# K and V of a batch pooled into one tile and turned in 128x128 shapes, two low weight pieces on GpSimd, another order of the two output scatters of a half block

## The chip, the core and the metric

The kernel runs on one core of a Trainium2 chip. The metric is the device time of one execution in microseconds (us). A core has five engines that work side by side: PE (TensorE, matrix products; its weight loads are shown apart as PEld), DVE (VectorE), ACT (ScalarE), POOL (GpSimd) and SP (SyncE, here only an issuer of transfers). DMA queues carry data between DRAM and the on-chip memory and inside it.

## The reference, cut to what matters

```python
q, k, v = (8, 8, 576, 64) each; moe_w_gate (512, 8), moe_w1 (8, 512, 1024), moe_w2 (8, 1024, 512)
k_p = k.reshape(B, H, 72, 8, D).mean(axis=3)          # 8 neighbours of the sequence pooled
v_p = v.reshape(B, H, 72, 8, D).mean(axis=3)
attn = softmax(q @ k_p^T / sqrt(D));  attn_out = attn @ v_p
x = attn_out.transpose(0, 2, 1, 3).reshape(4608, 512)  # one row per token, heads side by side
logits = x @ w_gate;  expert_idx = argmax(logits);  gate_w = softmax(logits)[expert_idx]
y[tokens of e] = relu(x[tokens of e] @ w1[e]) @ w2[e]  # each token by its one expert
return gate_w[:, None] * y
```

Inputs and output are float32. The kernel computes the products of the experts in pairs of float16 numbers, a high part and a low part (the rest after rounding), with three products for one.

## The kernel before

The program has two halves. The first is the attention with the router. It runs over 36 units of 128 tokens (four to a batch and one shared by the 64 left-over tokens of each pair of batches), in the loop at L1000 to L1045. In unit i the code lays down, in this order for every engine: GpSimd's hook "q"; the transposes of the probabilities (`u_pt`, L524 on PE, copied out by ACT as `pt`, L526); scores of a later unit (`g_s`, L500, or L494 where tokens of two batches meet) and their exponentials (`g_exp`, L517, ACT); transposes of q (`g_qt`, L477, copied by ACT L480); the hooks "pe", "act", "dve"; the product with V (`u_pv`, L546); small steps of the router from a list of fillers; the hooks "dve3", "pe2", "sp"; the moves inside the chip's memory, issued by ACT (L1037); and `u_nrm` (DVE L573, L574, L575), which divides by the sum of the exponentials and writes the token rows `both`. The engines take their instructions in this order, so the place of a hook is a place in a queue.

K and V of batch b are loaded by SP into one of three tiles `kv`, and GpSimd sums each over its 8 neighbours in three additions: 128x1280 (L338), 128x640 (L340), 128x320 (L341). Each L338, and each L340 that is placed alone, waits for the newest "beat", the reciprocal L574 of the unit laid down before (`on_beat`, L316). The table POOLAT gives the units. K then goes through PE (`k_pe`, L379) and ACT (`k_act`, L391) into the score operand `bd`, whose upper and lower 64 partitions hold the same numbers for different heads, so one half is written by ACT and the other is copied from it by a transfer that ACT's queue issues (L1037). V goes two ways: PE turns it (`v_pe`, L403 to L407), ACT copies it (`v_act`), PE multiplies it with the router's weights (`u_pe`, L422, L424), and DVE writes that product (`gates`, L431) and V itself under the mask `mk` (`masked`, L436, two instructions for one batch) into `vb`, the right operand of `u_pv`.

The other steps that the change touches: `lsplit` (L868) writes on DVE the low part of a piece of the first expert's weights, as four instructions of 128x256 for each of eight pieces j, at hook "dve3" of units 13 to 35. The router's rows of a group of four units are scattered by GpSimd to `x_by_expert` in DRAM, sorted by expert (L677, one indirect transfer per unit, held in a list and laid down one by one by `flush`). When the rows of the first 24 units are out, SP loads the first block of 256 rows (L927, unit 29), GpSimd splits it into high and low (L901, L902, unit 30), SP's transposing transfers turn it (L913, unit 31), and PE begins the first block's first product in units 33 to 35 (L987 to L989).

The second half is the expert layer: a loop over blocks of 256 rows (full) or 128 rows (half) of one expert, L1319. At a block's end ACT scales two results of 128 rows (`take`, L1273) and GpSimd scatters them to the output (`give`, L1276 to L1278), row set 1 first and row set 0 second. In a half block, row set 1 has no rows: its row numbers lie outside of the output and nothing is written.

## Time and profile before

| | us |
|---|---|
| median of 3 runs | 592.2 |
| lowest, highest run | 591.74, 595.24 |
| the profiled execution | 594.74 |
| its span, first to last instruction | 592.1 |
| PE busy in the span | 567.0 (96%) |
| DVE busy | 306.5 (52%) |
| ACT busy | 276.4 (47%) |
| POOL busy | 241.4 (41%) |
| mean granted clock of TensorE | 0.987 |

The profile is of one execution. The rows of a timeline give the start and the duration of an instruction or of a run of equal ones (xN), and in brackets how long the engine had been idle before it and what released it. A matmul's duration overlaps with the next one's, so PE's progress is read from starts. ACTq, SPq and POOLq rows are the issuing of transfers, not the transfers.

### The profile page before, as it was taken

What the parts mean: (1) busy time and instruction counts of PE and PEld (TensorE: products, weight loads), DVE (VectorE), ACT (ScalarE), POOL (GpSimd) and SP (SyncE); (2) the same over time, 40 slices, a digit from 0 to 9 for tenths busy, and PEclk for the clock granted to TensorE, in tenths of its full rate; (3) what the DMA queues carried; (4) which work ended last, traced back from release to release, by engine and by line L of the source; (5) the groups of instructions that cost most, each with busy time, mean ns of one, the idle gap of its engine ahead of it and who ended that gap; (6) DMA issues with size and microseconds to landing.
All of it is one profiled execution on the core that took longest, in us unless ns stands there. A gap on an engine that the chain in (4) does not pass through costs nothing. (4 is left out here: it accounts for less than half of the span.)

```text
span 592.1 us, 15018 instructions
## 1 busy us (share of the span) xinstructions
PE 567.0 (96%) x4332; PEld 423.3 (71%) x4333; DVE 306.5 (52%) x639; ACT 276.4 (47%) x627; POOL 241.4 (41%) x465
## 2 busy tenths in 40 slices
PE   7989999999999989999999999999999999999993
PEld 6778998889885755775676676765767657767571
DVE  5776779997798272128312221272313723182783
ACT  4666788878942362227222222261223622272771
POOL 6495889884545222122222012231122311224255
PEclk8998999999999999999999999999999999999998
DMA  9997999857357959952943214339143491319310
GB/s 278 299 313 196 327 336 344 255 173 277 98 187 230 287 154 360 347 123 65 335 134 91 53 58 111 90 66 351 58 111 84 95 352 38 105 35 333 75 45 12
DMA packets 94072, 107.76 MB, mean 182 GB/s; under 512 B 53894, under 2 KB 62086, under 8 KB 94040
## 3 DMA queue, kind: packets, MB, share of 16 engines
q1 hardware_dynamic: 86408, 85.46, 49.6%
q0 software_dynamic: 6640, 20.99, 9.5%
q10 hardware_dynamic: 992, 0.92, 0.6%
q8 instruction: 16, 0.26, 0.2%
q14 instruction: 16, 0.13, 0.1%
HBM read 73.65 MB, written 23.37 MB: 164 GB/s over the span
## 5 line engine op out<-in xcount | busy, mean ns | idle before, releaser
L1067 PEld LDWEIGHTS <-bd 128*128 128x128 f16 x936 | 91.2, 98 | 105.7 <-DVE bd L1061 0.8
L1061 DVE SCALAR_TENSOR_TENSOR bd<-ps,bd 128x512 f16<-128x512 f32 (+1 forms) x44 | 27.5, 630 | 143.7 <-ACT bd L1057 143.2
L1277 POOL TENSOR_TENSOR spacer<-ql,iG 1x1 f32<-1x1 f32 x44 | 18.5, 420 | 166.2 <-ACT ql L1273 154.1
L517 ACT ACTIVATE both<-ps,nmx 128x72 f32<-128x72 f32 x288 | 70.0, 350 | 12.6 <-DVE nmx L510 12.2
L1067 PE MATMUL po<-w,bd 128*128 128x512 f16 x264 | 59.1, 379 | 0.0
L1067 PE MATMUL po<-kv,bd 128*128 128x512 f16 x264 | 58.8, 379 | 0.0
L546 PE MATMUL po<-vb,pt 128*128 128x146 f32 (+1 forms) x320 | 52.7, 311 | 5.5 <-DVE both L575 4.6
L1278 POOL DMA_INDIRECT out_dram<-ql,iG x44 | 47.1, 1071 | 22.0 <-issue 20.6
L1057 ACT ACTIVATE bd<-ps 128x512 f16<-128x512 f32 (+1 forms) x44 | 23.8, 547 | 69.2 <-PE L987 56.4
L546 PEld LDWEIGHTS po<-vb,pt 128*128 128x128 f32 x320 | 46.5, 192 | 8.4 <-issue 5.2
L1067 PE MATMUL pq<-kv,bd 128*128 128x512 f16 x216 | 48.1, 379 | 0.0
L989 PE MATMUL ps<-kv,qt 128*128 128x256 f16 (+1 forms) x176 | 44.8, 263 | 0.9 <-DVE qt L115 0.9
L677 POOL DMA_INDIRECT x_by_expert<-both,rpos x36 | 35.8, 996 | 23.2 <-issue 6.2
L987 PE MATMUL ps<-kv,w 128*128 128x256 f16 (+1 forms) x176 | 43.1, 258 | 2.3 <-DVE bd L906 1.8
L500 PE MATMUL ps<-bd,qT 128*128 128x144 f32 x256 | 45.0, 301 | 0.0
L987 PE MATMUL ps<-kv,qt 128*128 128x256 f16 (+1 forms) x176 | 44.8, 263 | 0.0
L988 PE MATMUL ps<-kv,qt 128*128 128x256 f16 (+1 forms) x176 | 44.8, 263 | 0.0
L989 PE MATMUL ps<-kv,w 128*128 128x256 f16 (+1 forms) x176 | 43.1, 258 | 0.0
L988 PE MATMUL ps<-kv,w 128*128 128x256 f16 (+1 forms) x176 | 43.1, 258 | 0.0
L1067 PE MATMUL pq<-w,bd 128*128 128x512 f16 x192 | 42.7, 379 | 0.0
L338 POOL TENSOR_TENSOR st<-kv 128x1280 f32<-128x1280 f32 x13 | 37.7, 2901 | 12.0 <-DVE ri L574 7.0
L1273 ACT ACTIVATE ql<-po,gB 128x512 f32<-128x512 f32 x22 | 15.1, 685 | 55.5 <-PE L987 41.6
(246 smaller groups left out, 1274.4 us busy)
## 6 DMA issues: line engine op xcount, KB each, us to landing
st<-in_moe_w_dram SPq DMA_DIRECT2D x8, 2048.0 KB, 13.8
both<-in_moe_w_dram SPq DMA_DIRECT2D x6, 2048.0 KB, 12.9
vb<-x_by_expert SPq DMA_DIRECT2D x16, 578.0 KB
kv<-in_v_dram SPq DMA_DIRECT2D x16, 512.0 KB
kv<-in_k_dram SPq DMA_DIRECT2D x7, 1024.0 KB
qt<-in_q_dram SPq DMA_DIRECT2D x7, 1024.0 KB
st<-in_moe_w_dram SPq DMA_DIRECT2D x4, 1024.0 KB
kv<-in_v_dram SPq DMA_DIRECT2D x8, 208.0 KB
```

What stands on the lines that cost most here:

```text
L338: on_beat(nc.gpsimd.tensor_tensor(t1, src[:, :, 0:4 * D], src[:, :, 4 * D:], op=OP.add))
L500: nc.tensor.matmul(ps[:, x * 2 * KP:(x + 1) * 2 * KP], t[:, h, :], BD[b % 3][:, :, h, :], start=True, stop=True)
L517: nc.scalar.activation(p[:, h * KP:(h + 1) * KP], ps[:, x * KP:(x + 1) * KP], AF.Exp, bias=nmx[:, x:x + 1], scale=-1.0)
L546: nc.tensor.matmul(po[:, cols], a[:, c * 128:(c + 1) * 128], VB[b % 3][:, c, sl, 0:CW], start=h in (0, LEFT), stop=False, skip_group_check ...
L677: st = nc.gpsimd.indirect_dma_start(out=xs, out_offset=bass.IndirectOffsetOnAxis(ap=Z["pos"][:, u:u + 1], axis=0), in_=X[:, u, :], in_offs ...
L987: nc.tensor.matmul(dst, wh, xT[:, d, 0:n], start=(d == 0), stop=False)
L988: nc.tensor.matmul(dst, wh, xT[:, DC + d, 0:n], start=False, stop=False)
L989: nc.tensor.matmul(dst, wl, xT[:, d, 0:n], start=False, stop=(d == DC - 1))
L1057: nc.scalar.activation(h, p, AF.Relu)
L1061: V.scalar_tensor_tensor(l, p, 0.0, h, op0=OP.max, op1=OP.subtract)
L1067: nc.tensor.matmul(y, hT[x][:, f, 128 * j:128 * j + 128], W2[s][z][:, f, :], start=(half == x == z == f == 0), stop=(half == z == 1 and f ...
L1278: st = nc.gpsimd.indirect_dma_start(out=out, out_offset=bass.IndirectOffsetOnAxis(ap=iG[:, j:j + 1], axis=0), in_=ys[j], in_offset=None, b ...
```

## The change

Four things change.

First, K and V of a batch are pooled into one tile `kvp` of ten chunks of 128x64 (K in chunks 0 to 4, V in 5 to 9, the 104-row last chunk of V now first, so that K's last chunk and V's last chunk are neighbours). Two neighbouring chunks are turned as one 128x128 transpose. From batch 2 on, `k_pe` has two transposes in place of four, and `v_pe` has three in place of four (two full ones, one of 64 columns and one of 64x64). For K both halves of `bd` now get one half of their numbers from ACT (two copies of 64x2x128 in place of one of 64x512) and the rest by a transfer (two of 64x2x128 in place of one of 64x512); for V one ACT copy of 128x384 replaces one of 128x256 and one of 64x128.

Second, `masked` comes before `gates` on DVE. The two `masked` instructions of batch 1 join the list of beats; the first pooling addition of batch 2's V moves from hook "q" of unit 2 to hook "dve3" of unit 3, its second and third from unit 3 to unit 4. So this L338 now waits for the second `masked` of batch 1.

Third, the low parts of weight pieces 0 and 1 leave DVE (eight L868 at units 13 to 21) and become four GpSimd instructions of 128x1024 at hook "q" of units 24, 25, 27 and 28 (`gsplit`), each waiting for the newest beat.

Fourth, at the end of a half block the scatter of row set 0 comes first and the empty one second; a full block keeps its order. For this GpSimd loads one more register at the top of each turn and branches at its end.

```diff
-VK = (0, 128, 216, 344, 472)
+VK = (472, 0, 128, 216, 344)
...
     def k_pe(b):
-        kp = KVS["kp", b]
+        kp = KVS["kvp", b]
         pm = KVS["pk", b] = psA.tile([128, 512], F32, name="pq", bufs=2)
-        for c in range(4):
-            nc.tensor.transpose(pm[0:64, c * 128:(c + 1) * 128], kp[:, c], ident)
-        if b == 1:
+        if b > 1:
+            for x in range(2):
+                nc.tensor.transpose(pm[:, 128 * x:128 * x + 128], pair(kp, 2 * x), ident)
+        else:
+            for c in range(4):
+                nc.tensor.transpose(pm[0:64, c * 128:(c + 1) * 128], kp[:, c], ident)
...
     def k_act(b):
         pm = KVS.pop(("pk", b))
-        for s in range(2 if b == 1 else 1):
+        if b > 1:
+            for s in range(2):
+                nc.scalar.activation(other(b, s, s), pm[64 * s:64 * s + 64, 0:256].rearrange("p (a x) -> p a x", a=2),
+                                     AF.Copy, scale=-SC)
+                moves.append((other(b, 1 - s, s), other(b, s, s), b))
+            return
...
     def v_pe(b):
-        vp, kp = KVS["vp", b], KVS.pop(("kp", b), None)
+        kvp = KVS["kvp", b]
         pm = KVS["pv", b] = psA.tile([128, 512], F32, name="pq", bufs=2)
-        for c in range(2):
-            nc.tensor.transpose(pm[:, c * 128:c * 128 + 128], vp[:, 2 * c:2 * c + 2, :].rearrange("p c d -> p (c d)"),
-                                ident)
-        nc.tensor.transpose(pm[0:64, 256:384], vp[:, 4], ident)
-        if b > 1:
-            nc.tensor.transpose(pm[0:64, 384:448], kp[0:64, 4], ident[0:64, 0:64])
+        for x in range(3):
+            nc.tensor.transpose(pm[:, x * 128:x * 128 + 128], pair(kvp, 4 + 2 * x), ident)
...
-            if hi == 5:
+            if lo == 0:
                 laid.add(b)
+            if b == 1:
+                beat.append(done)
...
-        fillers[0:0] = [(-1, False, f) for f in (gates, masked_low, masked_high)]
+        fillers[0:0] = [(-1, False, f) for f in (masked_low, masked_high, gates)]
...
-                        put(POOLAT[b] + x + y, "q", f, b, y)
+                        put(*((3, "dve3") if (b, x, y) == (2, 2, 0) else (POOLAT[b] + x + y + (b == 2 and x == 2), "q")),
+                            f, b, y)
...
-    for j, at in enumerate(((13, 14, 15, 16), (18, 19, 20, 21), (22, 23, 24, 25), (27, 28, 29, 30), (31, 31, 32, 32),
-                            (32, 33, 33, 33), (33, 34, 34, 34), (34, 35, 35, 35))):
+    for j, at in ((2, (22, 23, 24, 25)), (3, (27, 28, 29, 30)), (4, (31, 31, 32, 32)), (5, (32, 33, 33, 33)),
+                  (6, (33, 34, 34, 34)), (7, (34, 35, 35, 35))):
         for x in range(4):
             put(at[x], "dve3", lsplit, j, x, 4)
+
+    def gsplit(j, part):
+        src, t = st1[0][:, j], scratch[j]
+        if part == 0:
+            on_beat(nc.gpsimd.tensor_tensor(t, src, swc[:, 0:1].to_broadcast([128, F]), op=OP.mult))
+        else:
+            on_beat(nc.gpsimd.tensor_tensor(W1[0][1][:, j], t, W1[0][0][:, j], op=OP.subtract))
+
+    for at, j, x in ((24, 0, 0), (25, 0, 1), (27, 1, 0), (28, 1, 1)):
+        put(at, "q", gsplit, j, x)
...
+        many = entry(4, t, [ENG.Pool], 0, 3)
...
-        give(1)
         for x in (0, 1):
             with tc.If(en3[x] > 0):
                 wwhole(en3[x], 1 - x)
         take(0)
-        give(0)
+        either(many > 1, lambda: [give(j) for j in (1, 0)], lambda: [give(j) for j in (0, 1)])
```

Three places of the programs are shown as the engines get them; lines of the change are numbered by its own file. The first is GpSimd at units 27 to 29, before: the last two scatters of the group of units 20 to 23, then the clearing of the tile `vb` into which the first block's rows are loaded.

```order
L677 DMA x_by_expert<-both,rpos 38016x578
L676 MEMSET spacer 1x1
L677 DMA x_by_expert<-both,rpos 38016x578
L234 MEMSET vb_162 128x1156
L235 MEMSET vb_162 128x2
```

The same place in the change, from the first half of weight piece 1 on.

```order
L896 TENSOR_TENSOR kv_153<-st_64,swc 128x1024
L688 MEMSET spacer 1x1
L689 DMA x_by_expert<-both,rpos 38016x578
L898 TENSOR_TENSOR w_01_61<-kv_153,w_00_60 128x1024
L688 MEMSET spacer 1x1
L689 DMA x_by_expert<-both,rpos 38016x578
L688 MEMSET spacer 1x1
L689 DMA x_by_expert<-both,rpos 38016x578
L688 MEMSET spacer 1x1
L689 DMA x_by_expert<-both,rpos 38016x578
L235 MEMSET vb_163 128x1156
L236 MEMSET vb_163 128x2
```

The scatter that stands between L896 and L898 is the first of that group; the other three now stand behind L898.

The second place is DVE in unit 3, where V of batch 1 is laid into `vb`, before.

```order
L510 TENSOR_REDUCE nmx<-ps 128x4 x2
L431 TENSOR_TENSOR vb_161<-pq,mk 128x15x8
L436 TENSOR_TENSOR vb_161<-vp,mk 128x3x2x64
L436 TENSOR_TENSOR vb_161<-vp,mk 128x6x64
L573 TENSOR_SCALAR ri<-po 128x8
```

The same place in the change.

```order
L522 TENSOR_REDUCE nmx<-ps 128x4 x2
L446 TENSOR_TENSOR vb_162<-kvp,mk 128x3x2x64
L446 TENSOR_TENSOR vb_162<-kvp,mk 128x2x3x64
L440 TENSOR_TENSOR vb_162<-pq,mk 128x15x8
L585 TENSOR_SCALAR ri<-po 128x8
```

The product with the router's weights (L431, now L440) has moved behind the two masked copies.

The third place is ACT in units 3 and 4, where K of batch 2 is written to `bd`, before.

```order
L391 ACTIVATE bd_159<-pq 64x512
L526 ACTIVATE pt<-pp 128x640
L517 ACTIVATE both<-ps,nmx 128x72 x4
L480 ACTIVATE qT<-pq 128x512
L517 ACTIVATE both<-ps,nmx 128x72 x4
L1037 DMA bd_159<-bd_159 64x512
L526 ACTIVATE pt<-pp 128x640
```

The same place in the change.

```order
L403 ACTIVATE bd_160<-pq 64x2x128 x2
L538 ACTIVATE pt<-pp 128x640
L529 ACTIVATE both<-ps,nmx 128x72 x4
L492 ACTIVATE qT<-pq 128x512
L529 ACTIVATE both<-ps,nmx 128x72 x4
L1063 DMA bd_160<-bd_160 64x2x128 x2
L538 ACTIVATE pt<-pp 128x640
```

One copy has become two, and one issue of a transfer ahead of the next `pt` copy has become two.

## Rows read from the trace of the kernel before

**Rows 1.** Windows: engines' busy us (instructions), granted clock, DMA share, GB/s.

```profile
44.80:48.20 3.40, 3.40 (x14) 3.34 (x14) 1.73 (x7) 2.29 (x9) 2.28 (x2) 0.50 1.07 264
48.20:130.00 81.80, 77.94 (x652) 72.05 (x651) 67.40 (x182) 63.32 (x217) 67.83 (x63) 1.00 0.89 276
130.00:176.00 46.00, 45.33 (x393) 41.83 (x392) 37.83 (x133) 34.76 (x110) 24.35 (x46) 1.00 0.54 178
225.00:580.00 355.00, 354.06 (x2668) 240.78 (x2667) 137.11 (x165) 129.62 (x179) 92.05 (x243) 1.00 0.48 144
```

**Rows 2.** Timeline of PE: start, us, instruction, idle before and its releaser.

```profile
44.63 2.86 PE L546 MATMUL po<-vb,pt 128*128 128x146 f32 x10 [2.51 <-DVE both L575]
53.41 0.66 PE L500 MATMUL ps<-bd,qT 128*128 128x144 f32 x4
...
131.28 0.60 PE L379 MATMUL pq<-ident,kp 128*64 128x128 f32 x4
131.71 1.54 PE L546 MATMUL po<-vb,pt 128*128 128x146 f32 x10
```

**Rows 3.** Timeline of DVE, the masked copies of batches 1 and 2.

```profile
38.39 4.99 DVE L436 TENSOR_TENSOR vb<-vp,mk 128x384 f32<-128x384 f32 x2
...
55.45 1.09 DVE L436 TENSOR_TENSOR vb<-vp,mk 128x384 f32<-128x384 f32 x2
```

**Rows 4.** Timeline of POOL, pooling of batch 2's V.

```profile
38.25 2.90 POOL L338 TENSOR_TENSOR st<-kv 128x1280 f32<-128x1280 f32 x1
...
43.04 1.06 POOL L341 TENSOR_TENSOR vp<-st 128x320 f32<-128x320 f32 x1
```

**Rows 5.** Timelines of ACT's and SP's queues, the copies inside `bd`.

```profile
46.06 0.55 ACTq L1037 DMA_DIRECT2D bd<-bd  x1
...
44.09 9.57 SPq L270 DMA_DIRECT2D ql<-in_q_dram  x2
...
75.54 0.47 ACTq L1037 DMA_DIRECT2D bd<-bd  x1
76.05 0.70 ACT L526 ACTIVATE pt<-pp 128x640 f32<-128x640 f32 x1 [0.55 <-PE pp L524]
```

**Rows 6.** Waits of PE, 48 to 165: total us, times, longest.

```profile
PE po L546 <- DVE both L575: 2.1, 3, 1.0
PE pq L379 <- DVE rt L660: 0.9, 1, 0.9
```

**Rows 7.** Line L868: durations min/median/max ns, first and last start.

```profile
L868 DVE SCALAR_TENSOR_TENSOR w<-st,w x32: 394/416/1611, 88.2 to 174.6; 128x256 f16<-128x256 f32 x32
```

**Rows 8.** Timelines of DVE and POOL, scatters and the split.

```profile
145.99 0.20 DVE L574 RECIPROCAL ri<-ri 128x8 f32<-128x8 f32 x1
153.04 0.20 DVE L574 RECIPROCAL ri<-ri 128x8 f32<-128x8 f32 x1
...
140.39 0.96 POOL L677 DMA_INDIRECT x_by_expert<-both,rpos  x1 [5.67 <-DVE both L673]
...
144.20 0.97 POOL L677 DMA_INDIRECT x_by_expert<-both,rpos  x1 [0.23 <-issue]
...
153.38 1.03 POOL L901 TENSOR_TENSOR bd<-vb,zf 128x512 f16<-128x512 f32 x1 [6.97 <-ACT both L517]
```

**Rows 9.** Landing of L677's transfers, 139.5 to 145.2 and 160 to 166.

```profile
DMA to landing us min/median/max: 3.7/4.4/5.1
...
DMA to landing us min/median/max: 2.9/3.1/3.2
```

**Rows 10.** Timelines of SP and PE: load, turning and first product of block 0.

```profile
148.97 0.37 SPq L927 DMA_DIRECT2D vb<-x_by_expert  x1
155.69 3.65 SPq L913 DMA_TRANSPOSE kv<-bd  x2
...
165.16 0.27 PE L987 MATMUL ps<-kv,w 128*128 128x256 f16 x1
```

**Rows 11.** Landing of L1278's two transfers of the last block, 583 to 592.

```profile
DMA to landing us min/median/max: 2.1/2.2/2.3
```

## What the change should do to the time

> **What bounds the kernel now.** I read the windows first [rows 1]. In the expert layer PE is busy 354.06 of 355.00 us at full clock, so nothing that the change does to other engines can show there except at its very end. In the attention from 48.2 to 130 PE is busy 77.94 of 81.80 us, and from 130 to 176 45.33 of 46.00: PE is the bound, with some 4 us of stalls. The one bad stretch is 44.8 to 48.2, where PE was granted 0.50 of its clock, the lower of its two levels (1.2 GHz).
>
> The timeline of PE says why [rows 2]: the product with V at 44.63 had stood still for 2.51 us for DVE's L575, and the half clock follows. On DVE the two masked copies of batch 1 took 4.99 us there; for batch 2 the same two took 1.09 [rows 3]. In those 4.99 us GpSimd pooled batch 2's V, L338 from 38.25 and the last addition's end at 44.10 [rows 4]. So DVE's copies and GpSimd's additions shut each other out, and DVE, with everything behind it, came last.
>
> By the Trainium skill ("SBUF — State Buffer", "Who interferes with whom") a DVE instruction with two inputs in that memory and a GpSimd instruction that reads it share a port as an exclusive lock, held for the whole instruction. The 4.99 against 1.09 agrees. By that rule each added GpSimd reader of the change can hold DVE for its full length, which is a loss and is weighed at the weight pieces below.
>
> In the waits of PE from 48 to 165 [rows 6] DVE stands first: 2.1 us in three waits for `both`, 0.9 for the router's L660.
>
> **The change, part by part.** The sum is made against the profiled span of 592.1 us.
>
> *Order of masked copies and pooling (units 2 to 4).* DVE's copies no longer queue behind the router's product and GpSimd's L338 waits for them, so they take about the 1.09 us of batch 2 from about 38.3, and L575 comes 3.9 us earlier than it did. PE's stall of 2.51 goes: +2.5. Without the stall I expect no fall of the clock: the 3.40 us at 0.50 are 1.70 us of work at full clock, +1.7. GpSimd starts V of batch 2 at about 39.3 instead of 38.25; its three additions took 5.85 us with the collision, so V is there at about 45, and the turned V is first wanted at about 45.6 on the shortened time line. That cover is thin (0.6 us); if it is gone, the excess is paid on PE one for one. What is late next is K of batch 3, whose additions stand behind V of batch 2 on GpSimd and meet batch 2's masked copies, which before ran alone at 55.45: -0.2 (0 to -2, by the 3.9 that one collision cost, of which PE saw 2.5).
>
> *Fewer transposes.* Four turns of K took 131.28 to 131.71 on PE, 0.43 us [rows 2], 0.108 each. Each batch from 2 on loses two of K and one of V: 0.32 us, for six batches 1.9 us where PE is the bound. For batch 2's and batch 3's K and V I count all (+0.5); of the later ones, in which the next product waited for DVE or GpSimd anyway, I count three K and two V (+0.9). Bounds 0.9 to 1.9; I take 1.4. The wider operand costs PE nothing that I can see, since a turn's output has as many columns as before. ACT's two copies of 64x2x128 move half of the columns each, so ACT's copying is no longer.
>
> *One more transfer per K.* ACT issues 18 in place of 12. An issue takes 0.47 us [rows 5] and stands ahead of `pt`: at 75.54 the issue ended just as PE handed over, and `pt` began at 76.05. A second one pushes `pt` by 0.47 and, if nothing else waits, the product with V as well. Six batches: 0 to -2.8. For batches 2 and 3 the move lies in a unit that waits for DVE less than before, for later ones three of the moves lie ahead of a `pt` that PE waits for: with 0.3 us of each reaching PE, -1.0. Queued behind are the exponentials, which wait for PE in any case.
>
> The transfers must also land. In the trace of before the one copy of batch 2 was issued at 46.06, and SP, whose second load of the left-over q at 44.09 had to wait for it, was done with issuing at 53.66 [rows 5], so the copy took about 6.5 to 7 us. Its first reader, the scores at 53.41 [rows 2], moves forward to about 48.7 by the gains above. ACT can now issue the two from about 42.1 on (before, its exponentials stood behind the same stall), which puts the landing at 48.6 to 49.5. Cost 0 to -2, taken -0.7.
>
> *Weight pieces on GpSimd.* Eight L868 leave DVE. Their least time is 0.39 us each and their longest 1.61 [rows 7], where GpSimd was reading. Together with the gates now last (which puts the router's product behind 1.09 us of copies in units in which PE is not far), I take +0.5 out of the 3.0 us of PE's waits for DVE, bounds 0 to 3.0. On GpSimd a piece is two instructions of 128x1024: between twice the 1.03 us of a 128x512 [rows 8] and four fifths of the 2.90 of a 128x1280 [rows 4], so 2.06 to 2.32, taken 2.2. They start on a beat, so beside L575; the router's small steps and the masked copies of batch 7 come behind it. If each of four were to hold DVE once for its length that is 8.8 us on an engine that is busy 37.8 of 46.0 [rows 1]; little of it reaches PE: -0.4, bounds 0 to -2.
>
> *Scatters pushed back.* The last half of piece 1 waits for the beat at 145.99 and ends at 146.2 + 2.2 = 148.4; three scatters stand behind it. Four took from 140.39 to 144.20 [rows 8], 1.27 apart, so the last starts at about 151.2 where it started at 144.20: 7 us later. They landed 3.7 to 5.1 us after their start there, 2.9 to 3.2 in a quieter stretch [rows 9]; so at 154.1 to 156.3. Only then can SP load block 0's rows (before at 148.97 [rows 10]). The load had landed by 153.38, when GpSimd began the split, but the split then waited for the beat at 153.04, so the load had at most 4.4 us, and I take about 3. The split thus begins at 157 to 160, 4 to 7 us later than before. Before, SP had issued the turning transfers by 155.69 + 3.65 = 159.34 and PE's first product at 165.16 found them landed without a wait; with about 1.5 us of landing (estimated from the 2.1 us that a whole transfer takes in rows 11, part of it issuing) the slack is some 4.3 us. So the block's rows are late by -0.5 to +2.7 us; I count -0.3, bounds 0 to -3, and up to -1.7 more if the clock falls again as it did after 44.63.
>
> *Order at the end.* GpSimd generates both transfers one after the other and the program ends with the later; the empty one took as long as the full one (2.1 and 2.3 us [rows 11]). So the order changes nothing at the end, and the added register load and branch cost some tenths: -0.2 (-0.6 to +0.3).
>
> The sum: 2.5 + 1.7 - 0.2 + 1.4 - 1.0 - 0.7 + 0.5 - 0.4 - 0.3 - 0.2 = +3.3. Span 588.8. The profiled execution (594.74) is 2.5 over the median of the runs (592.2), so the gain is taken off the median: 592.2 - 3.3 = 588.9.
>
> **Rivals.** *A: the first block is late (the other side).* At PE's L987, units 33 to 35. If the scatters land as slowly as at 140 to 144 [rows 9], PE stands 2.7 us and its clock is halved for a stretch like 44.8 to 48.2, 1.7 more; add the second issue's full 2.8 and the sum is 3.3 + 0.3 - 4.4 - 1.8 = -2.6, 594.8; with the issue as above it is -0.8, 593.0. It decides from the point at which the rows reach PE 3 us after it asks. Against it: the queue is emptier after 150. Chance 0.17.
>
> *B: DVE's relief is the larger part.* PE's 3.0 us of waits for DVE [rows 6] go as a whole, the extra issues hide behind PE's own work, all 1.9 us of transposes count: 3.3 + 2.5 + 1.0 + 0.5 + 0.7 = 8.0, 584.2. For it: the two longest entries among PE's waits name DVE. Against it: removing one wait mostly bares the next. Chance 0.15.
>
> *C: the early gain is not had.* Either V of batch 2 or the copies of its K come 2.5 us late, so the stall moves to unit 5 or 6 and the clock falls there: 3.3 - 2.5 - 1.7 + 0.7 = -0.2, 592.4. This is also what it would look like if the collision were only moved. Chance 0.12.
>
> **How the numbers follow.** The forecast holds 0.56. Its own range, with each term near its value, is 587 to 591. The range reaches to rival A at 593 and to the middle of B at 585; about 2 in 10 lie outside of it. About one per cent, 6 us, is what a measurement of this kernel can tell from no change. Faster than 586.3 needs B or most of it: 0.17. Slower than 598.1 needs A, C and the full price of issues together: 0.03. Between: 0.80.
>
> **What would show it right or wrong.** The masked copies of batch 1 at about 1.1 us for two, no granted clock below 1.00 between 41 and 49, and no long stall of the product with V after unit 3. A wait of the scores of unit 6 for the copies within `bd`, under 1 us. `pt` beginning half a microsecond after PE's hand-over in units with two moves. The scatters of units 21 to 23 ending about 7 us later against the beats, and PE's first product of block 0 in unit 33 waiting less than 1 us. The two last scatters in the other order with the end as far behind the last product as now. I am wrong if the half clock stays in units 3 to 6, if it comes back in unit 33, or if PE's idle time between 48 and 165 shrinks by more than 2 us.

## The result, and the profile after

The changed kernel took 601.25 us (median of 4 runs, 600.67 to 602.11) where the kernel before took 593.19 beside it. The ratio is 1.0137, with a 95% interval of 1.0107 to 1.0167. So it is slower by 1.4%, some 8 us. I had forecast 588.9 with a range of 585.0 to 593.0. A second measurement on another chip (kernel change_again, below) gave 1.0099 [1.0061, 1.0138].

The windows of the changed kernel, with the columns of [rows 1], show the first thing that I was right about and the first that I missed.

```profile
44.80:48.20 3.40, 3.40 (x33) 3.04 (x32) 2.82 (x6) 2.81 (x11) 3.32 (x3) 1.00 0.95 298
48.20:130.00 81.80, 74.37 (x612) 69.19 (x611) 64.64 (x170) 61.22 (x210) 68.40 (x63) 0.98 0.89 274
130.00:176.00 46.00, 42.83 (x370) 39.90 (x370) 37.87 (x128) 35.17 (x111) 30.64 (x46) 1.00 0.51 159
225.00:580.00 355.00, 354.05 (x2673) 241.54 (x2671) 134.89 (x160) 129.27 (x179) 91.67 (x244) 1.00 0.48 146
```

The half clock at 44.8 to 48.2 is gone. But PE is now busy 74.37 us of the next 81.80 where it was 77.94, and 42.83 of 46.00 where it was 45.33. It has more stalls, not fewer, and the clock of this stretch is 0.98: a half clock has come at a new place (below).

DVE's masked copies of batch 1 take 1.02 us for two, where [rows 3] had 4.99:

```profile
39.34 1.02 DVE L446 TENSOR_TENSOR vb<-kvp,mk 128x384 f32<-128x384 f32 x2
```

In the timeline of PE the stall has moved to unit 6, to the scores that read the copied half of batch 2's K (L512, which was L500 at 53.41 in [rows 2]). Behind it the product with V takes 2.76 us for ten, about what it took at 44.63 in [rows 2] with half the clock, and the granted clock, 0.86 on average from 48.2 to 60 us, is 0.61 from 54 to 58.

```profile
51.16 0.48 PE L512 MATMUL ps<-bd,qT 128*128 128x144 f32 x2 [0.77 <-DMA bd<-bd]
52.40 0.51 PE L512 MATMUL ps<-bd,qT 128*128 128x144 f32 x2 [0.76 <-DMA bd<-bd]
...
54.58 2.76 PE L558 MATMUL po<-vb,pt 128*128 128x146 f32 x10
```

```profile
48.20:60.00 11.80, 10.23 (x72) 9.14 (x72) 8.41 (x23) 6.61 (x24) 7.87 (x6) 0.86 0.97 252
```

The waits of PE from 48 to 165 (total us, times, longest; [rows 6] before) are now headed by ACT's copy `pt`:

```profile
PE po L558 <- ACT pt L538: 3.6, 6, 1.1
PE po L558 <- DVE both L587: 2.4, 3, 1.2
PE ps L512 <- DMA bd<-bd: 1.5, 2, 0.8
PE pq L660 <- DVE vb L440: 1.2, 1, 1.2
```

At the end, the timeline of POOL and one row of ACT show the two scatters of the last, half block. The empty one waits for the transfer of the first (1.48 us), and ACT's copy of the last block waits for GpSimd, which had been held in the same way in the block before (1.78 us, the first row).

```profile
584.16 1.20 POOL L1302 TENSOR_TENSOR iG<-iB,zi 128x2 int32<-128x2 int32 x1 [1.78 <-DMA out_dram<-ql,iG]
...
588.40 0.69 ACT L1299 ACTIVATE ql<-po,gB 128x512 f32<-128x512 f32 x1 [4.91 <-POOL iC L905]
...
590.43 1.00 POOL L1304 DMA_INDIRECT out_dram<-ql,iG  x1 [0.57 <-issue]
592.90 0.18 POOL L1302 TENSOR_TENSOR iG<-iB,zi 128x2 int32<-128x2 int32 x1 [1.48 <-DMA out_dram<-ql,iG]
593.16 0.18 POOL L1303 TENSOR_TENSOR spacer<-ql,iG 1x1 f32<-1x1 f32 x1
593.90 1.00 POOL L1304 DMA_INDIRECT out_dram<-ql,iG  x1 [0.56 <-issue]
```

To see where 7.1 us of span went I cut each profiled execution at the starts of the units' reciprocals (L574 before, L586 after, read from the timeline of DVE) and of the last first-layer product (L987, L1013; in the other kernels the same instructions under their own line numbers). A stage is the difference of two such starts. The table holds the first profile of before, a second one (before_again, below), the change, and three kernels of the experiments.

| stage, us | before | before again | change | give_as_before | k_pairs_apart | best_again |
|---|---|---|---|---|---|---|
| start to unit 0 | 26.20 | 28.10 | 28.06 | 27.15 | 27.55 | 26.11 |
| units 2 to 3 | 8.10 | 5.67 | 4.34 | 4.34 | 4.34 | 4.34 |
| units 3 to 5 | 8.99 | 7.34 | 9.02 | 9.90 | 9.03 | 9.91 |
| units 5 to 6 | 5.41 | 6.52 | 6.98 | 8.52 | 6.55 | 5.19 |
| units 6 to 12 | 24.84 | 24.85 | 25.29 | 25.51 | 25.24 | 24.67 |
| units 12 to 23 | 47.32 | 47.31 | 47.41 | 47.38 | 47.42 | 47.25 |
| units 23 to 32 | 34.82 | 34.81 | 35.31 | 35.45 | 35.08 | 34.72 |
| units 32 to 33 | 3.38 | 3.39 | 4.70 | 4.47 | 4.34 | 4.16 |
| unit 35 to the last L987 | 402.37 | 401.98 | 403.33 | 403.42 | 402.74 | 402.36 |
| from there to the end | 14.59 | 14.58 | 18.68 | 14.56 | 14.57 | 14.67 |
| span | 592.1 | 590.6 | 599.2 | 596.8 | 593.0 | 589.5 |

(Units 0 to 2 take 9.18 and units 33 to 35 take 6.93 in all six.) Against the first profile of before the change gains 3.76 in units 2 to 3. It loses 1.86 at the start, 1.57 in units 5 to 6, 0.45 + 0.09 + 0.49 up to unit 32, 1.32 in units 32 to 33, 0.96 over the expert layer's loop and 4.09 at the end. That makes up the 7.1. Against the second profile of before, whose start is as late, nothing is gained up to unit 6 (20.34 us for units 2 to 6 against 19.53), and the change is 8.6 us longer. So the gain of 3.76 is one against a single execution.

### The profile page after: what moved, and what is told of

It is laid out like the page before. It is cut to its first block, busy times and chain, and to the rows that moved or that the text cites. A ratio compares the mean times of both kernels' runs of the same rounds, so it can differ in the third digit from the quotient of the medians.

```text
span 599.2 us, 15144 instructions
## 1 busy us (share of the span) xinstructions
PE 565.8 (94%) x4314; PEld 423.5 (71%) x4315; DVE 304.2 (51%) x631; ACT 276.7 (46%) x623; POOL 249.1 (42%) x472
## 3 DMA queue, kind: packets, MB, share of 16 engines
q10 hardware_dynamic: 2240, 0.92, 0.7%
## 5 line engine op out<-in xcount | busy, mean ns | idle before, releaser
L558 PEld LDWEIGHTS po<-vb,pt 128*128 128x128 f32 x320 | 47.7, 197 | 9.3 <-ACT pt L538 6.3
L1013 PE MATMUL ps<-kv,w 128*128 128x256 f16 (+1 forms) x176 | 43.1, 258 | 4.7 <-ACT kv L113 2.7
L512 PE MATMUL ps<-bd,qT 128*128 128x144 f32 x256 | 45.1, 301 | 1.5 <-DMA bd<-bd 1.5
L1015 PE MATMUL ps<-kv,qt 128*128 128x256 f16 (+1 forms) x176 | 44.8, 263 | 0.9 <-DVE qt L115 0.9
L1013 PE MATMUL ps<-kv,qt 128*128 128x256 f16 (+1 forms) x176 | 44.8, 263 | 0.0
L1299 ACT ACTIVATE ql<-po,gB 128x512 f32<-128x512 f32 x22 | 15.1, 685 | 59.0 <-PE L1014 42.9
```

Source lines behind the costliest of these rows:

```text
L512: nc.tensor.matmul(ps[:, x * 2 * KP:(x + 1) * 2 * KP], t[:, h, :], BD[b % 3][:, :, h, :], start=True, stop=True)
L558: nc.tensor.matmul(po[:, cols], a[:, c * 128:(c + 1) * 128], VB[b % 3][:, c, sl, 0:CW], start=h in (0, LEFT), stop=False, skip_group_check ...
L1013: nc.tensor.matmul(dst, wh, xT[:, d, 0:n], start=(d == 0), stop=False)
L1015: nc.tensor.matmul(dst, wl, xT[:, d, 0:n], start=False, stop=(d == DC - 1))
```

## The experiments

All kernels of one set ran on one chip, beside the kernel before. Ratios are to before on that chip.

**give_column**: each scatter writes its own column of the row numbers.

```diff
-        nc.gpsimd.tensor_tensor(iG[:, 0:j + 1], iB[:, 0:j + 1], zi.to_broadcast([128, j + 1]), op=OP.add)
+        nc.gpsimd.tensor_tensor(iG[:, j:j + 1], iB[:, j:j + 1], zi, op=OP.add)
```

> The change, with one edit: each output scatter writes only its own column of the row numbers iG (before it writes all columns up to its own). In the changed kernel's trace GpSimd's L1302 of the second, empty scatter of a half block waits 1.78 and 1.48 us for the first scatter's transfer, and ACT's last copy waits behind it. Theory (a false dependence: the second write of iG overlaps the column that the first transfer still reads): those waits are gone, the last scatter starts about 3.6 us behind the last matmul as before, the time falls by 3 to 4 us, to about 597.5. Rival (the order itself is what costs, since the empty transfer's generation now comes last): waits gone, but the end stays as far behind the last matmul; 600 to 601.

Measured: 1.0051 [1.0011, 1.0091]; tail_turn_last, which keeps the wide write, had 1.0104 beside it, with an interval that overlaps. The timeline of POOL at its end:

```profile
592.66 1.00 POOL L1304 DMA_INDIRECT out_dram<-ql,iG  x1 [0.58 <-issue]
593.68 0.21 POOL L1302 TENSOR_TENSOR iG<-iB,zi 128x1 int32<-128x1 int32 x1
593.97 0.18 POOL L1303 TENSOR_TENSOR spacer<-ql,iG 1x1 f32<-1x1 f32 x1
594.70 1.00 POOL L1304 DMA_INDIRECT out_dram<-ql,iG  x1 [0.56 <-issue]
```

The wait of 1.48 us is gone, and the last stage is 15.15 us in place of 18.68. In all five profiles here with the wide write in the new order that stage took 18.7 to 18.8 us, in all others 14.6 to 15.6. So most of the loss was a false dependence. `give(1)` writes columns 0 and 1. As the first of the two that does no harm, because the transfer behind it reads column 1 and the next write is to column 0 alone. As the second it overwrites column 0, which the transfer ahead of it still reads, and has to wait until that has landed.

**tail_turn_last**: batch 0's three turns of V in the order second, third, first.

```diff
-        for x in range(3):
+        for x in ((1, 2, 0) if b == 0 else (0, 1, 2)):
```

> The change, with one edit: the three turns of batch 0's V go in the order second, third, first, so that the one with the tail chunk, which is pooled last, comes last. In the changed kernel's trace PE stands 1.32 us for that chunk at 19.39 and has half its clock soon after; unit 0's beat is 1.86 us later than before the change. Theory (the turn that needs the last pooled chunk heads the queue): PE's wait at the start falls under 0.7 us, the clock of 20 to 27 us is higher, unit 0's beat comes 1.2 to 1.9 us earlier; the time falls by about as much unless a later stall takes it. Rival (the start differs by loads or by the added clearing of tiles): no change of unit 0's beat, 601.

Measured: 1.0104 [1.0065, 1.0144], as the change itself. Unit 0's reciprocal stood at 26.37 us. In give_column, without this edit, it stood at 25.99. The late start of the change's profile, 28.06, was not the change's doing. It goes with a half clock from 20 to 27 us, and the second profile of before (before_again) has both, with a start of 28.10. The window in the change:

```profile
20.00:27.00 7.00, 7.00 (x33) 6.81 (x32) 4.42 (x7) 2.99 (x10) 2.34 (x3) 0.55 1.08 298
```

and in before_again:

```profile
20.00:27.00 7.00, 7.00 (x30) 6.57 (x29) 4.39 (x6) 2.88 (x11) 2.83 (x3) 0.52 1.07 310
```

Over all kernels here the start took 23.6 to 29.7 us.

**k_turned_by_64**: K of batches 2 to 7 turned, copied and moved as before the change.

```diff
-        if b > 1:
-            for x in range(2):
-                nc.tensor.transpose(pm[:, 128 * x:128 * x + 128], pair(kp, 2 * x), ident)
-        else:
-            for c in range(4):
-                nc.tensor.transpose(pm[0:64, c * 128:(c + 1) * 128], kp[:, c], ident)
+        for c in range(4):
+            nc.tensor.transpose(pm[0:64, c * 128:(c + 1) * 128], kp[:, c], ident)
+        if b == 1:
...
-            for s in range(2):
-                nc.scalar.activation(other(b, s, s), pm[64 * s:64 * s + 64, 0:256].rearrange("p (a x) -> p a x", a=2),
-                                     AF.Copy, scale=-SC)
-                moves.append((other(b, 1 - s, s), other(b, s, s), b))
+            nc.scalar.activation(half(b, 0)[:, 0:512], pm[0:64, :], AF.Copy, scale=-SC)
+            moves.append((half(b, 1)[:, 0:512], half(b, 0)[:, 0:512], b))
             return
```

> The change, with K of batches 2 to 7 turned as before it: four turns of 64 columns, one ACT copy of 64x512, one transfer of 64x512 inside bd instead of two of 64x2x128 (V's three full turns and the common tile stay). In the changed kernel's trace the scores of unit 6 wait 0.77 and 0.76 us for these transfers, half clock follows (a product with V of 2.76 us at 54.58), and the product with V waits 3.6 us in all for pt. Theory 1 (two transfers in pieces of 512 bytes land later and their issues hold ACT): those waits fall to under 0.5 and about 1.5 us, the clock stays at 1.00 there, and units 6 to 32 gain 2 to 4 us net of 1.3 us more of turns on PE; time 597 to 599. Rival (any copy of K lands late, once the first stall is gone): the wait of unit 6 stays at 1.5 us or more, 600 to 602.

Measured: 1.0003 [0.9964, 1.0042], about 1% less than tail_turn_last beside it. Units 5 to 6 took 5.68 us (7.47 in tail_turn_last), units 6 to 32 107.14 (108.01 in the change's profile, 108.41 in tail_turn_last). The wait for `bd` was not among PE's, those for `pt` fell to 0.8, and the granted clock of 48.2 to 60 was 1.00 (0.86 in tail_turn_last). Theory 1 holds for the waits and the clock; in units 6 to 32 it had 2 to 4 us of gain, and they gained 0.9 to 1.3.

**pieces_on_dve**: the low parts of weight pieces 0 and 1 back on DVE at units 13 to 21, no `gsplit`.

> The change, with the low parts of weight pieces 0 and 1 back on DVE (eight instructions at units 13 to 21) and no weight piece on GpSimd. In the changed kernel's trace PE waits 1.5 us for block 0's turned rows at unit 33, and ACT and DVE reach the expert layer about 1 us later. Theory (the second half of piece 1 holds three scatters behind the beat of unit 27, so the rows come late): the wait in unit 33 is gone and the expert layer starts 1.3 to 2.4 us earlier; DVE's waits in units 13 to 21 grow by 0.3 to 1 us; time 599.5 to 600. Rival (the rows are late because the whole attention is): the wait stays over 1 us, and the time is 601 or more.

Measured: 1.0119 [1.0030, 1.0209] from 4 runs, so no gain is seen. PE no longer waited for `kv<-bd`, but units 12 to 23 took 48.12 us (47.41 in the change) and units 23 to 32 took 38.64 (35.31). The first goes with longer waits of PE for `both` (5.0 us, 2.4 in the change); that `gates`, now last and with DVE's pieces beside it, causes them is my reading. The second I can't explain (below).

**change_again**: the changed kernel once more, with the three that follow.

> The changed kernel as it is, once more, beside the kernel before and the three below on one chip. Expected ratio to before 1.010 to 1.017 as in the first measurement; the half clock at 20 to 27 us may or may not come again (in three kernels with the same wait of 1.3 us for the last pooled chunk it came in one), so unit 0's beat at -0.2 to +1.9 us against before.

Measured: 1.0099 [1.0061, 1.0138]. Unit 0 came at 24.60, without a half clock at 20 to 27 us.

**k64_and_column**: k_turned_by_64 and give_column together.

> The change with two edits: K of batches 2 to 7 turned, copied and moved as before it (four turns of 64, one transfer of 64x512), and each output scatter writing its own column of iG alone. Theory (the two K transfers and the false dependence are the losses, each 4 to 5 us, and they add): ratio to before 0.990 to 0.998, the last scatter again about 3.6 us behind the last matmul, no wait for bd at unit 6. Rival (they overlap, since a late loss hides an early one): ratio 1.000 to 1.004.

Measured: 0.9895 [0.9835, 0.9954] from 5 runs, last stage 15.29. Against change_again it is 2% less, so the two losses add. How far below the kernel before it lies is less sure: nearly the same kernel on another chip (k64_column_tail_last, below) had 0.9978.

**k64_column_pieces**: the same with the weight pieces back on DVE.

> As k64_and_column, and the low parts of weight pieces 0 and 1 back on DVE. Theory (late rows of block 0, 1.3 us at unit 33, come from the scatters behind the second half of piece 1): no wait of PE for kv<-bd at unit 33, 1 to 2 us less than k64_and_column. Rival (DVE's relief in units 13 to 21 is worth more than the late rows cost): 1 to 2 us more than k64_and_column, with longer waits for both and rt.

Measured: 0.9988 [0.9954, 1.0022]. The time is the rival's, 0.9% more than k64_and_column, with PE's waits for `both` at 5.3 us and a wait of 1.5 for `rt`. Its cause is only in part: units 12 to 23 took 0.9 us more (48.23 against 47.30), but units 23 to 32 took 2.7 more (37.36 against 34.70), with the unexplained step of pieces_on_dve.

**order_alone**: the kernel before with the second part of the change alone (masked copies first, batch 1's as beats, V of batch 2 pooled later).

> The kernel before with one part of the change: masked copies ahead of gates on DVE, batch 1's masked copies as beats, and batch 2's V pooled from unit 3's hook dve3 on. Theory (the early stall and the half clock behind it are worth 3.8 us and nothing takes them back): 2.5 to 4 us less than before, ratio 0.993 to 0.996, masked copies of batch 1 at about 1.1 us for two. Rival (the one transfer of K, issued at the same place but wanted earlier, is late at unit 6): the gain falls under 1.5 us, with a wait of L500 for bd.

Measured: 0.9987 [0.9955, 1.0019]. Units 2 to 3 took 4.57 and units 5 to 6 5.19, as the theory has it (the masked copies took 1.75 us for two, where it had 1.1). But units 12 to 23 took 47.91 (47.31 before) and the loss in units 23 to 32 is here as well (37.42), so the gain that the theory had in the time, 2.5 to 4 us, isn't there.

**before_again**: the kernel before, profiled a second time.

> The kernel before, profiled on the chip of the other runs. Ratio 1.000. In three kernels with all weight pieces on DVE the units 24 and 27 took 2.2 and 1.2 us longer than in the first profile of before, with PE's semaphores late in a burst. Theory (it belongs to DVE's pieces on this chip): it is here too, beat of unit 24 about 2 us later against unit 23 than in the first profile. Rival (it needs the earlier attention of the other kernels): not here.

Measured: 0.9993 [0.9959, 1.0027]. The step of unit 24 is not here; but this set ran on another chip than the last, so neither theory is settled by it. It shows something else. The timeline of DVE for the masked copies of batch 1, to be held against [rows 3]:

```profile
40.27 2.56 DVE L436 TENSOR_TENSOR vb<-vp,mk 128x384 f32<-128x384 f32 x2
```

The collision cost 1.5 us here in place of 3.9, PE did not stand at the next product with V, and units 2 to 6 took 19.53 us in place of 22.50.

**pieces_alone**: the kernel before with the third part of the change alone (`gsplit`).

> The kernel before with one part of the change: the low parts of weight pieces 0 and 1 as four GpSimd instructions at units 24 to 28, eight DVE instructions fewer. Theory 1 (k64_and_column against k64_column_pieces: the move to GpSimd is worth 0.9%): ratio 0.989 to 0.994. Theory 2 (my forecast: DVE's relief 0.5 us, late rows -0.3): ratio 0.999 to 1.002. In both, block 0's rows are ready 4 to 7 us later against the beats, and PE's wait for them at unit 33 is under 1 us, as the attention here is later.

Measured: 1.0005 [0.9973, 1.0038]. Units 12 to 23 took 46.55 (47.31), units 23 to 32 35.28 (34.81), units 32 to 33 3.97 (3.39). What the first stage gains (0.76) is given back where GpSimd splits the pieces and where block 0's rows are late (0.47 and 0.58), and nothing is left that can be measured. Theory 2, my forecast, holds.

This kernel runs batch 1's masked copies in the order of before, and in its profile they hardly met GpSimd at all:

```profile
36.45 1.21 DVE L436 TENSOR_TENSOR vb<-vp,mk 128x384 f32<-128x384 f32 x2
```

Units 2 to 3 took 4.58 us, as in order_alone with the new order (4.57). So three executions of the same early code had 4.99, 2.56 and 1.21 us for these two copies.

**k64_give_as_before**: k64_and_column with the loop's end as before the change, and the own-column edit taken back.

```diff
+        give(1)
         for x in (0, 1):
             with tc.If(en3[x] > 0):
                 wwhole(en3[x], 1 - x)
         take(0)
-        either(many > 1, lambda: [give(j) for j in (1, 0)], lambda: [give(j) for j in (0, 1)])
+        give(0)
```

> As k64_and_column, but with the loop's end as before the change (row set 1 first, its scatter ahead of the last copy, no branch) in place of the own-column edit. Theory (the new order gains nothing by itself, the empty transfer takes as long as the full one): 0 to 0.6 us less than k64_and_column, last scatter 3.6 us behind the last matmul. Rival (the real rows leaving first shortens the end): 0.5 to 1.5 us more.

Measured: 0.9936 [0.9903, 0.9969], last stage 15.02, 0.3 us less than in k64_and_column, as the theory has it.

**k64_column_tail_last**: k64_and_column with tail_turn_last.

> As k64_and_column, and batch 0's turn with the tail chunk last of the three. Theory (the 1.3 us wait for that chunk matters only where the clock falls behind it): unit 0's beat within the spread of the other kernels (-2 to +3.5 us against before), time within 2 us of k64_and_column. Rival (it is the cause of the late start): 1.3 to 2 us less, ratio 0.986 to 0.988.

Measured: 0.9978 [0.9945, 1.0010], last stage 15.28, unit 0 at 28.41. The turn's place is not the cause of the late start. Against k64_give_as_before on the same chip it is 0.4% more, with intervals that overlap. The new order without the false dependence has last stages of 15.1 to 15.6 us in four kernels, the old order 14.6 to 15.0 in nine profiles, so some tenths are its own cost.

**give_as_before**: the change with the fourth part undone alone.

> The change with its fourth part undone: the loop's end as before (row set 1's scatter ahead of the last copy, then row set 0). Theory (the order lets the second scatter's row numbers wait for the first transfer): the end behind the last up matmul is 14.6 to 15.1 us as before, where the change has 18.7; ratio to before 1.002 to 1.006. Rival (the gain of the own-column edit was chance): 1.010 or more.

Measured: 1.0087 [1.0058, 1.0115], last stage 14.56 as before the change. The end is the theory's; the time lies between the theory's 1.002 to 1.006 and the rival's 1.010, and the interval reaches into the first. Undoing the fourth part is seen in the stage, and not clearly in the time, since the change itself ran on other chips (1.0137, 1.0099). This kernel is the base of the next.

**k_pairs_apart**: give_as_before, with K's chunks loaded so that a turned pair holds chunks x and x+2. ACT's copy and each of the two transfers then have 64x256 in one stretch, rows of 1024 bytes in place of 512. The edit also loads K from DRAM in two transfers of 512 KB where it was one of 1024 KB, so the row length is not all that differs.

```diff
+        if b > 1:
+            for x in range(2):
+                nc.sync.dma_start(dst[:, 2 * x:2 * x + 2, :],
+                                  src[b, 0:512, :].rearrange("(a c p) x -> p c a x", a=2, c=2)[:, x])
...
-        return half(b, s)[:, 0:512].rearrange("p (a c x) -> p a c x", a=2, c=2)[:, :, c]
+        return half(b, s)[:, 256 * c:256 * c + 256]
```

> As give_as_before, but K of batches 2 to 7 loaded so that a turned pair holds chunks x and x+2: ACT writes 64x256 in one stretch and each of the two transfers has rows of 1024 bytes in place of 512. Theory 1 (short rows make the transfers late): landing and the wait of unit 6's scores for bd fall by more than half, that unit gains 1 to 2.5 us; the waits for pt stay. Theory 2 (the second issue on ACT and its place are the loss): unit 6 as in give_as_before (7 us and more from unit 5's beat), waits for pt as there. k64 has 5.2 us for that unit.

Measured: 1.0057 [1.0022, 1.0093]. The line of the transfers' issues (durations min/median/max in ns) and their landing, for give_as_before:

```profile
L1063 ACTq DMA_DIRECT2D bd<-bd x18: 492/597/1035, 43.2 to 142.2; - x18
DMA to landing us min/median/max: 3.7/7.4/8.8
```

for k_pairs_apart:

```profile
L1066 ACTq DMA_DIRECT2D bd<-bd x18: 468/469/673, 43.7 to 139.4; - x18
DMA to landing us min/median/max: 6.7/6.8/6.9
```

and the scores of unit 6 on PE, in give_as_before:

```profile
51.21 0.48 PE L512 MATMUL ps<-bd,qT 128*128 128x144 f32 x2 [1.73 <-DMA bd<-bd]
52.87 0.85 PE L512 MATMUL ps<-bd,qT 128*128 128x144 f32 x2 [1.18 <-DMA bd<-bd]
```

in k_pairs_apart:

```profile
50.48 0.73 PE L515 MATMUL ps<-bd,qT 128*128 128x144 f32 x4 [0.59 <-DMA bd<-bd]
```

Both theories hold a part. An issue on ACT costs 0.47 in place of 0.60. The wait for `bd` falls from 2.9 us to 0.6 (0.8 to 2.9 in the six kernels with rows of 512 bytes), and units 5 to 6 take 2.0 us less than in give_as_before. But those six kernels took 6.24 to 8.88 us for these units, so 6.55 is within their spread, and the time, 1.0057 against 1.0087, has intervals that overlap. The landing settles nothing: the trace knows it for only four of the 18 transfers of give_as_before and two of k_pairs_apart. Those of 64 KB landed 6.5, 8.4 and 8.8 us after their issue in the first and 6.7 in the second; the shortest, 3.7, and the 6.9 are small transfers of 16 KB. PE's waits for `pt` stay, at 2.9 us against 3.6, and best_again beside it, with one transfer, has 0.6 of them and runs 1% faster than k_pairs_apart.

**best_again**: k64_give_as_before once more.

> The same kernel as k64_give_as_before, once more: the change with K turned by 64 and the loop's end as before. Expected ratio 0.990 to 0.997 again; units 3 to 6 in 18.6 to 19.5 us with no wait for bd.

Measured: 0.9960 [0.9925, 0.9995]. Twice measured, this version beats the kernel before, by 0.4 and 0.6%. It also beats the change: the intervals of both (0.9903 to 0.9995) lie below the change's (1.0061 to 1.0167).

**best_pieces_sooner**: best_again with `gsplit` at units 24, 25, 25 and 26.

> As best_again, with the weight pieces on GpSimd at units 24, 25, 25 and 26 in place of 24, 25, 27 and 28, so that the last four scatters of rows 0 to 23's group stand behind no beat of unit 27. Theory: they end 2.5 us or more earlier against the beats, and units 32 to 33 take 3.4 us as before the change in place of 3.9; 0.3 to 0.8 us less in all, which only the stages can show. Rival (the rows are not what PE waits for there): 3.9 us again.

Measured: 0.9966 [0.9941, 0.9992]. The scatters did move ahead of unit 27's beat, but landed later, 2.9 to 5.3 us after their start where best_again has 2.9 to 3.9, and SP loaded the rows at 150.11 against 150.44. Units 32 to 33 took 4.17 where best_again beside it has 4.16, and the time is the same: the rival's outcome. This kernel, with one transfer for K, also had a granted clock of 0.60 in units 5 to 6 and took 6.92 us for them, behind a wait of 2.6 us for ACT's copy of q.

## Why the prediction was wrong, step by step

*The end: a step that failed.* I took the order at the end for -0.2 us (-0.6 to +0.3), reasoning from the length of the two transfers ([rows 11]) and from nothing else. I had the line of code in front of me that writes `iG[:, 0:j + 1]`, and did not ask what the second write waits for when its order is turned. It waits for the first transfer to land, and GpSimd's next instructions and ACT's copy wait behind it: 4.09 us in the last stage, outside of my bounds. Shown by give_column and give_as_before: without the wide write, or with the old order, the stage is back at 15.15 and 14.56 us.

*One more transfer per K: the right mechanism, far too small.* This is the larger failure. I had -1.0 for the issues and -0.7 for the landing, with bounds of -2.8 and -2. The issues: I took 0.47 us for one from the 64x512 copy. The median issue of the change takes 0.60, and a pair took 1.30 at one of the later units, where PE then stood 0.81 us. I also held that ACT's copying would be no longer: its two copies took 0.80 us there, where the one of 64x512 took 0.60. From the start of the copying to the start of `pt` ACT took 1.77 us where it had taken 1.15 ([rows 5] has the `pt` of before), 0.6 us more (timelines of ACT before, then of ACT and PE of the change):

```profile
74.90 0.60 ACT L391 ACTIVATE bd<-pq 64x512 f32<-64x512 f32 x1
```

```profile
74.80 0.80 ACT L403 ACTIVATE bd<-pq 64x256 f32<-64x256 f32 x2
75.22 1.30 ACTq L1063 DMA_DIRECT2D bd<-bd  x2
76.57 0.70 ACT L538 ACTIVATE pt<-pp 128x640 f32<-128x640 f32 x1 [0.97 <-PE pq L489]
...
77.33 1.64 PE L558 MATMUL po<-vb,pt 128*128 128x146 f32 x10 [0.81 <-ACT pt L538]
```

PE's waits for `pt` are 3.6 us in six waits, against 0.6 with one transfer (best_again). They grew by 3.0 us where I had let 0.3 us of each of three moves reach PE: that is the step of this term that failed. Units 6 to 32 took 108.00 to 109.14 us in the five kernels with two transfers of 512-byte rows and the pieces on GpSimd, and 106.50 to 107.14 in the six with one. The landing: in best_again, with the same early gain, units 5 to 6 take 5.19, in the change 6.98 and in give_as_before 8.52, part of it the clock, which falls behind the stall as it did at 44.63 in [rows 2]. This place is not the two transfers' alone: k64_column_tail_last and best_pieces_sooner, with one, took 7.05 and 6.92 there, also with a clock under 1.00 (0.76 and 0.60). I had seen that risk as rival C, but priced it from 6.5 to 7 us of landing for all transfers; of the three of 64 KB whose landing the change's trace knows, the latest took 8.7 us, and the one of batch 2, for which unit 6 waits, 7.4. In all, K's two transfers cost what give_as_before and best_again differ by, 1.3% on one chip, some 7.5 us with the saved turns already taken off, where the two terms had 1.7. How that divides into issues, copies and landing is not shown.

*Fewer transposes: not visible.* I had +1.4. In best_again, with four turns for K, units 6 to 12 take 24.67, less than the 25.24 to 25.51 of the kernels with two. I read it so that PE's turns were saved where PE then waited for ACT; no run separates the two.

*The early stall: right in mechanism, sized from one execution.* The masked copies, the stall and the half clock went as forecast, 3.76 us in units 2 to 3 (I had 4.2 with the clock). But the size of that stall is chance: a second execution of before had 1.5 us of collision and no half clock at 44.8 to 48.2, and pieces_alone, with the same early code, had 0.1 us and units 2 to 3 as short as with the new order. My reading is that it hangs on when GpSimd's addition starts against DVE. Measured over runs, this part of the change alone gave 0.9987 [0.9955, 1.0019], with the open loss in units 23 to 32 (below) in it. A loss of one profiled execution was counted as a loss of the median.

*Weight pieces and late rows.* For these I had +0.5, -0.4 and -0.3, about nothing in sum, and pieces_alone gave 1.0005. Within the change the rows came as forecast up to the load (the last scatter ended at 152.58, the load began at 154.64, in the forecast 154.1 to 156.3), but SP's issuing of the turning transfers then took 4.81 us where it had taken 3.65 ([rows 10]), and PE waited 1.5 us, within my bounds (timelines of POOL, SP and PE).

```profile
146.73 2.13 POOL L898 TENSOR_TENSOR w<-kv,w 128x1024 f16<-128x1024 f32 x1 [0.96 <-DVE ri L586]
...
151.61 0.97 POOL L689 DMA_INDIRECT x_by_expert<-both,rpos  x1 [0.23 <-issue]
...
154.64 0.37 SPq L953 DMA_DIRECT2D vb<-x_by_expert  x1
160.84 4.81 SPq L939 DMA_TRANSPOSE kv<-bd  x2
...
167.21 0.27 PE L1013 MATMUL ps<-kv,w 128*128 128x256 f16 x1 [1.55 <-DMA kv<-bd]
```

These are rival A's mechanism at half of its price: units 32 to 33 took 1.32 us more, and the granted clock stayed at 1.00 from 165 to 182 us. The two instructions of piece 1 took 1.89 and 2.13 us, where I had 2.2 for each.

*What stays open.* The 0.96 us over the expert layer's loop is in the kernels with two transfers for K (403.33, 403.42) and not in best_again (402.36); but order_alone, with K as before, took 404.8 there and k_turned_by_64 403.1, so it isn't shown to come from that part. The 1.86 us at the start are no part of the change, as far as the spread of the starts tells. And on the chip of order_alone and that of pieces_on_dve, kernels with all weight pieces on DVE lost 2.2 us at unit 24 and more than 1 us at unit 27. This is unit 24 in order_alone, on DVE and PE:

```profile
131.33 0.17 DVE L575 TENSOR_SCALAR ri<-po 128x8 f32<-128x8 f32 x1 [2.13 <-PE pq L654]
...
127.28 1.53 PE L548 MATMUL po<-vb,pt 128*128 128x146 f32 x10
...
132.67 1.61 PE L548 MATMUL po<-vb,pt 128*128 128x146 f32 x10 [1.78 <-DVE both L577]
```

DVE waited for the product of 127.28, which by PE's rows had ended more than two microseconds earlier. before_again, on another chip, does not have it, and no run settles whether it is the chip or the kernel. All kernels of these two sets also took 8.2 to 9.7 us for units 33 to 35 where those of the table took 6.9. That one is not the kernel alone: the change itself took 6.9 in its first profile and 9.7 in change_again.

## What to carry to other kernels

When two steps change places, read what each writes, not only how long it takes: a write that is wider than it needs to be is free in one order and a wait for a whole transfer in the other. A transfer inside the chip's memory also has an issue on some engine's queue (here 0.47 to 0.60 us on ACT), so halving PE's turns of K at the price of a second transfer lost here, where that queue feeds PE. And before a stall of one profiled execution is counted as a gain, a second execution should show the same stall.

## What the runs showed of the hardware that was not expected

The issue on ACT's queue of a transfer inside `bd` takes longer when its rows are cut in two: medians of 0.60 us for 64 rows of two stretches of 512 bytes (give_as_before) and 0.47 for one stretch of 1024 bytes (k_pairs_apart) or of 2048 (best_again). The queue made 2240, 1472 and 992 packets for the same 0.92 MB (part 3 of the page). The Trainium skill ("DMA: Bandwidth & Descriptors", "Why small descriptors are slow (HBM only)") says that transfers within that memory don't suffer from small descriptors. No run here settles that: the six landings of 64 KB with rows of 512 bytes that the profiles of the change and of give_as_before know are spread from 5.4 to 8.8 us, with loads from DRAM in flight beside them, and of those with rows of 1024 bytes only one is known, 6.7.

The start of the kernel, up to the first unit's reciprocal, varied from 23.6 to 29.7 us between the profiled executions, and not by kernel: the kernel before alone had 26.20 and 28.10.
